# Softmax weights of a recurrent-memory transformer: one Exp after the sums, and another place for the first half's weights

## The chip, the cores and the metric

The kernel runs on one core of a Trainium2 chip. The metric is the device time of one execution in microseconds (us), lower is better. Of the engines, TensorE (PE, with its weight loads PEld) multiplies matrices, VectorE (DVE), ScalarE (ACT) and GpSimd (POOL) work on tiles, and SyncE (SP) issues DMAs.

## The reference

Two branches start from the layer-normalised input `xn` (2048 tokens of 1024 values). One is a dense GELU network. The other is an attention that goes through the tokens in 64 segments of 32, each with 8 memory tokens in front that are the output of the segment before:

```python
for s in range(n_seg):                      # 64, each needs the memory of the one before
    h = concatenate([mem, xs], axis=1)      # 8 + 32 tokens
    q, k, v = h @ Wq, h @ Wk, h @ Wv        # 32 heads of 128
    scores = where(mask, q @ k.T * Dh ** -0.5, -1e9)
    p = softmax(scores)
    o = (p @ v) @ Wo
    mem = o[:, :M]                          # 8 rows go on to the next segment
    outs.append(o[:, M:])
return x + A_ref(xn, ...) + B_ref(xn, w1, b1, w2, b2)
```

## The kernel before, in words

The GELU network comes first (some 340 us). Then 64 segments follow one another, some 21 us each. A segment takes all of Wq, Wk, Wv and Wo, cut into 64 units of 512 KB. Of these, 47 stay in SBUF; 17 are brought anew in each segment, 15 by a DMA from HBM (`Wc_*`, issued by SyncE at line 286) into six slots in turn, and 2 by VectorE, which copies them out of PSUM banks where they are kept (`copy_bits`, line 275). When a streamed unit's products are done, `unit_done` starts the next one in its slot. The order in which streamed and resident units alternate is written out by hand (`PLACED`), for four kinds of segment, `i4 = s % 4`.

A segment goes through half passes of eight units: K0, Q0, K1, Q1, V0, V1 (0 and 1 are the halves of the 32 heads), and then 16 units of Wo. 24 of a segment's tokens and the 8 memory rows are multiplied by each unit (`product`, line 832, four matmuls of 512 columns on TensorE's four column groups). The last 8 tokens of four segments are gathered and multiplied once in four segments; such a pass (`left`) takes two products per unit. They fall on K in i4 = 0, V0 in 1, Q0 and V1 in 2, Q1 and Wo in 3.

The attention's steps are put between units of the passes, each after the unit that a table names, by i4:

- `scores(u)` (lines 945 and 951): the first half's after unit `SCORES_0` of K1, the second half's in `attend`, after unit `ATTEND` of V1. The scores stand in the PSUM bank `mixed`: 160 columns (4 heads of a partition group by 40 queries, part A) and 64 columns (the keys of the gathered tokens, part B).
- `exps(u)`: ScalarE's Exp, and VectorE's minimum with two masks that hold 0 or 3e38 (lines 969 and 970).
- `sums(u)`, after unit `SUMS_0` of Q1 and `SUMS_1` of V1: TensorE sums the weights of a head over its keys and spreads the sum (978, 984); ScalarE takes Ln (989) and then Exp of the negative (992), which is the sum's reciprocal. Two heads share a matmul of `values`, so the weights are laid out as pairs in which the other head's places are zero. Before, the zero comes out of the second Exp: it runs twice, with a bias `off` of 0 or -30000 for each partition. VectorE then multiplies (1000 for A, into `pd_main`; 1004 for B).
- `values(u, rs)`, after unit `VALUES_0` of V1 and `VALUES_1` of Wo (1019, 1025, copied out at 1038).

The queries of a half are copied and transposed by `turn_q` (916 by ScalarE, 920 by VectorE, in two parts of eight heads) and `q_left` (928) into `q_home`, 640 columns of the tile `kq`. The first half's weights after Exp stand in columns 400 to 624 of the same place, so the second half's queries must wait for line 1004. At the end of Wo, in segments without gathered rows, `fold` adds the halves of a bank (1084 to 1086), line 1190 adds the rest, `put_mem` (329, 339) brings the 8 memory rows into the next segment's tokens, and four to six products of a gathered pass (`lead_products`) lie beside that.

Of the kernel before, what the change touches and what calls it, by code (L numbers as in the profile page):

```python
# [11 lines left out]
U32 = mybir.dt.uint32  # L12
F32 = mybir.dt.float32
ACT = mybir.ActivationFunctionType
# [16 lines left out]
INV_SQRT_DH = 1.0 / math.sqrt(DH)  # L31
EPS = 1e-5
PASSED = 3.0e38
NEVER = -30000.0

# [18 lines left out]
EARLY_SEGS = 7  # L56
LEAD_FIRST = 4
SCORES_0 = (6, 6, 6, 6)
SUMS_0 = (4, 4, 4, 4)
ATTEND = (0, 0, 1, 0)  # L60
VALUES_0 = ((4, 4), (4, 4), (3, 5), (4, 4))
SUMS_1 = (6, 6, 5, 7)
VALUES_1 = (5, 5, 5, 5)
LATER = 4
LAG = 3
# [55 lines left out]
def kernel(  # L121
# [62 lines left out]

    homes = [hr_home[:, 0:256], hr_home[:, 256:512]]
    small_consts = consts.tile([P, 16], BF16, name="small_consts")
    bd, off = small_consts[:, 0:4], small_consts[:, 4:8].bitcast(F32)

    def slab(place):
        if place in low:  # L190
# [6 lines left out]
    ident_mem = nc.alloc_sbuf_tensor_at("ident_mem", [P, 4, NL], BF16, offset=SCRATCH + 3712)[:, :, :]  # L197
    nc.vector.tensor_copy(out=ident_mem[:, :, :], in_=ident.rearrange("p (j t) -> p j t", j=4)[:, :, NX:SEG])
    nc.vector.memset(bd[:, :], 0.0)
    nc.vector.memset(off[:, :], NEVER)  # L200
    for j in range(4):
        q = slice(32 * j, 32 * j + 32)
        nc.vector.memset(bd[q, j:j + 1], 1.0)
        nc.vector.memset(off[q, j % 2:j % 2 + 1], 0.0)


    mask = qL[1].rearrange("p h t -> p (h t)")[:, 0:NX + GRP * 16]
# [65 lines left out]
    def copy_bits(out, in_):  # L273

        nc.vector.tensor_single_scalar(out=out, in_=in_, scalar=0, op=ALU.bitwise_or)  # L275

    def start_stream(slot):
        if not starts:
            return
        n = starts.popleft()  # L280
        unit, t = streams[n], slab(slot)
        if unit in kept_in:
            for c0, bank in kept_in[unit]:
                copy_bits(t[:, c0:c0 + 1024].bitcast(U32), bank.bitcast(U32))
        elif unit in copies:
            nc.sync.dma_start(out=t[:, :], in_=copies[unit])
        else:
            fetch(t[:, :], unit)
        stream_tiles[n], slot_of[n] = t, slot
# [447 lines left out]
    with tc.tile_pool(name="late", bufs=1) as late:  # L737
# [65 lines left out]
        for s in range(NSEG):  # L803
# [14 lines left out]
            left_v = [first or i4 == 1, first or i4 == 2]  # L818
            left_o = i4 == 3
            mover = nc.vector if s < EARLY_SEGS else nc.gpsimd  # L820
            st = {}

            def product(w, i, t, lhs, acc, seq, left=False):
                for j in range(4):
# [111 lines left out]
            def scores(u):  # L936
# [12 lines left out]
                for j in range(4):  # L949
# [3 lines left out]
                        start=False, stop=True, skip_group_check=True, tile_position=(0, 32 * j),  # L953
                    )

            def exps(u):

                if u:
                    prA = q_all[:, 512:672].rearrange("p (c q) -> p c q", q=40)
                    prB = ko_slots[1][:, 0:64, i4]  # L960
                    nc.scalar.activation(out=q_all[:, 512:672], in_=mixed[:, 0:160], func=ACT.Exp, scale=INV_SQRT_DH)
                    nc.scalar.activation(out=prB, in_=mixed[:, 160:224], func=ACT.Exp, scale=INV_SQRT_DH)  # L962
                else:
                    pr = q_all[:, 400:624]
                    nc.scalar.activation(out=pr, in_=mixed[:, 0:224], func=ACT.Exp, scale=INV_SQRT_DH)
                    prA = pr[:, 0:160].rearrange("p (c q) -> p c q", q=40)
                    prB = pr[:, 160:224]
                p = prA[:, :, NL:SEG]
                nc.vector.tensor_tensor(out=p, in0=p, in1=mask_order[:, None].to_broadcast(list(p.shape)), op=ALU.min)  # L969
                nc.vector.tensor_tensor(out=prB, in0=prB, in1=mask_left, op=ALU.min)  # L970
                st["pr", u] = prA, prB.rearrange("p (c a q) -> p c a q", a=2, q=NL)

            def sums(u):
                prA, prB = st["pr", u]
                dA = mixed[:, 0:160].rearrange("p (c q) -> p c q", q=40)
                for j in range(4):
                    q = slice(32 * j, 32 * j + 32)
                    nc.tensor.matmul(
                        dA[q, :, :], lhsT=bd[:, j:j + 1].to_broadcast([P, 32]), rhs=prA, start=True, stop=False,
                        skip_group_check=True, tile_position=(0, 32 * j),  # L980
                    )
                for j in range(4):
                    q = slice(32 * j, 32 * j + 32)
                    nc.tensor.matmul(
                        ends(dA[q, :, :]), lhsT=bd[:, j:j + 1].to_broadcast([P, 32]),
                        rhs=prB,
                        start=False, stop=True, skip_group_check=True, tile_position=(0, 32 * j),
                    )
                nc.scalar.activation(out=mixed[:, 0:160], in_=mixed[:, 0:160], func=ACT.Ln)

                for b in (1, 0):
                    nc.scalar.activation(  # L992
                        out=mixed[:, 160 * b:160 * b + 160], in_=mixed[:, 0:160], func=ACT.Exp, scale=-1.0,
                        bias=off[:, b:b + 1],
                    )
                pdA = pd_main.rearrange("p (c b q) -> p c b q", c=4, b=2)
                place = qL_slots[0] if first or VALUES_0[i4][0] < VALUES_0[i4][1] else ko_slots[0]
                pdB = q_all[:, 512:640] if u else place[:, :, i4]
                dd = mixed[:, 0:320].rearrange("p (b c q) -> p b c q", b=2, q=40)
                nc.vector.tensor_tensor(  # L1000
                    out=pdA.rearrange("p c b q -> p b c q"), in0=prA[:, None, :, :].to_broadcast([P, 2, 4, 40]),
                    in1=dd, op=ALU.mult,
                )
                nc.vector.tensor_tensor(
                    out=pdB.rearrange("p (c b a q) -> p b c a q", c=4, b=2, q=NL),
                    in0=prB[:, None, :, :, :].to_broadcast([P, 2, 4, 2, NL]),
                    in1=dd.rearrange("p b c (e q) -> p b c e q", q=NL)[:, :, :, ::4, :], op=ALU.mult,
                )
                st["pd", u] = pdA, pdB

            def values(u, rs):

                V, (pdA, pdB) = st["V", u], st["pd", u]
                av = {r: new_acc() for r in rs}
                oV = {r: av[r][:, 0:320].rearrange("p (c b q) -> p c b q", c=4, b=2) for r in rs}
                for c in range(4):
                    for r in rs:
                        q = slice(64 * r, 64 * r + 64)
                        nc.tensor.matmul(  # L1019
                            oV[r][:, c, :, :], lhsT=V[q, c * P:(c + 1) * P], rhs=pdA[q, c, :, :],  # L1020
                            start=(c == 0), stop=False, skip_group_check=True, tile_position=(64 * r, 0),
                        )
                for r in rs:
                    q = slice(64 * r, 64 * r + 64)
                    nc.tensor.matmul(
                        av[r][:, 0:320].rearrange("p (n e q) -> p n e q", n=8, q=NL)[:, :, ::4, :],
                        lhsT=VL[u][q, i4 * P:(i4 + 1) * P], rhs=pdB[q, :].rearrange("p (n a q) -> p n a q", n=8, q=NL),
                        start=False, stop=True, skip_group_check=True, tile_position=(64 * r, 0),
                    )
                for r in rs:  # L1030
                    cp = nc.vector.tensor_copy if r else nc.scalar.copy
                    h = slice(8 * r, 8 * r + 8)
                    parts = [
                        (ko[u].rearrange("p h (t s) -> p h t s", s=GRP)[:, h, :, i4], 0, NL),
                        ((outM if u else nat_home)[:, h, :], NL, 40),
                    ]
                    for out, q0, q1 in parts:
                        cp(out=out.rearrange("p (b c) q -> p c b q", b=2), in_=oV[r][:, :, :, q0:q1])  # L1038
                    let_go(av[r])
# [39 lines left out]
            def fold(ps):  # L1079
# [2 lines left out]

                here, there = [ps[:, 256 * b:256 * b + 256].rearrange("p (h e) -> p h e", e=16) for b in range(2)]
                nc.scalar.copy(out=t[0:64], in_=there[64:128])
                nc.vector.tensor_copy(out=t[64:128], in_=there[0:64])
                nc.vector.tensor_tensor(out=t[:, :, :], in0=here, in1=t[:, :, :], op=ALU.add)
                let_go(ps)
                return t
# [26 lines left out]
            at = {  # L1115
                0: [lambda: nc.vector.transpose(out=nat_home, in_=nat_home)],
            }
            at[4 if first else SUMS_0[i4]] = [lambda: sums(0)] + ([] if left_q[1] else [lambda: q_left(1)])
            if left_k[1]:
                at.setdefault(1, []).insert(0, lambda: turn_kL(psK1L, 1))  # L1120
            psQ1, psQ1L = half_pass("Q", 1, left_q[1], at, lambda ps: turn_qL(ps, 1))
# [19 lines left out]
                st["V", 0] = values_out(psV, v_home, nc.scalar.copy)  # L1141
                exps(1)

            at = {0 if first else ATTEND[i4]: [attend]}
            n0, n1 = (3, 5) if first else VALUES_0[i4]
            if n0 == n1:
                at.setdefault(n0, []).append(lambda: values(0, (0, 1)))
# [15 lines left out]
                load_left_rows(g + 2, left_rows_in[:, :])  # L1163
            at = {VALUES_1[i4]: [lambda: values(1, (0, 1))]}
            psX = new_acc()
            for n, unit in enumerate(O_UNITS):
                t = unit_tile(unit)
                if n == NPAIR and not left_o:
# [3 lines left out]
                unit_done(unit)  # L1172
                for fn in at.get(n, ()):
                    fn()
                if n == 6 and left_o:
                    st["resL"] = pd_main[:, 0:256]
                    loads.dma_start(
                        out=st["resL"], in_=resL_d[g, :, :]
                    )
# [94 lines left out]
```

## Time and profile before

| what | value |
|---|---|
| time, median of 3 runs | 1776.12 us (1768.8 to 1776.93) |
| profiled execution: its own time | 1779.09 us |
| profiled execution: span | 1777.4 us |
| TensorE busy | 1690.2 us (95%), 28374 matmuls |
| VectorE busy | 1020.6 us (57%), 2592 instructions |
| ScalarE busy | 697.1 us (39%), 1743 instructions |
| DMA moved | 593.82 MB, mean 334 GB/s over the span |
| granted TensorE clock | 0.999 |

The span goes from the first to the last instruction. Lines of the profile name an engine, a line of the kernel (L1000 is line 1000), an operation and `out<-in` by the program's names. In an order of time each line has the start and the duration in us, and in square brackets the idle time before it and what ended it. A line of waits has who waited for whom, the total in us, the number of times and the longest.

### The profile page before, as it was taken

Reading aid. Unit: us, or ns where it says so; the run is one execution under the profiler, and the core shown is the slowest. Engines: PE = TensorE matmul, PEld = TensorE weight load, DVE = VectorE, ACT = ScalarE, POOL = GpSimd, SP = SyncE. Lnnn points to the kernel's source line nnn. Section 1 sums busy time; section 2 is a strip of 40 time slices with the busy share of each in tenths; the row PEclk is TensorE's granted clock in tenths of the full one; section 3 lists DMA queues with packets and bytes.
Section 4 is the critical chain, followed back from the end, with each engine's and each line's share of the span. In section 5 each row is a group of like instructions: output and inputs, shape, how many; then the busy total and the mean of one; then the engine's idle time right before and its main releaser. Section 6 shows DMA issues by size and latency. Waiting matters only on the chain.

```text
span 1777.4 us, 65923 instructions
## 1 busy us (share of the span) xinstructions
PE 1690.2 (95%) x28374; PEld 834.6 (47%) x28374; DVE 1020.6 (57%) x2592; ACT 697.1 (39%) x1743; POOL 293.0 (16%) x590
## 2 busy tenths in 40 slices
PE   9999999998999999999999989999999999999998
PEld 5444444444444444444444444444444444444444
DVE  7657483826556555555556555555565655565554
ACT  6334251703334343334334433433333434333333
POOL 0000002403120111121211212121212111111120
PEclk9999999999999999999999999999999999999999
DMA  9455312779999999999999999999999999999997
GB/s 273 152 165 173 97 37 64 275 268 349 380 384 395 381 389 387 388 388 392 381 385 393 384 386 363 400 370 397 384 399 376 396 384 402 378 387 390 395 382 293
DMA packets 233752, 593.82 MB, mean 334 GB/s; under 512 B 58003, under 2 KB 88771, under 8 KB 233460
## 3 DMA queue, kind: packets, MB, share of 16 engines
q1 hardware_dynamic: 199680, 568.05, 84.5%
q0 software_dynamic: 16160, 15.82, 2.8%
q10 hardware_dynamic: 17620, 5.74, 1.3%
q8 instruction: 222, 3.64, 0.8%
q14 instruction: 70, 0.57, 0.1%
HBM read 573.22 MB, written 28.70 MB: 339 GB/s over the span
## 4 chain that ended last, share of the span: by engine, by line
PE 41%; DMA 25%; DVE 5%; ACT 3%; issue 1%; ACTq 0%; DVEq 0%; SPq 0%
PE acc L832 27%; PE acc L1069 11%; DMA u<-Wc_O 11%; DMA u<-Wc_Q 7%; DMA u<-Wc_V 4%; DMA u<-Wc_K 2%; PE acc L1019 1%; DVE kq L920 1%; ACT mixed L992 1%; DMA hr_home<-res_d 1%; ACT qL L886 1%; PE mixed L945 1%; DVE pd_main L1000 1%; PE mixed L329 1%; DVE kq L1190 0%
## 5 line engine op out<-in xcount | busy, mean ns | idle before, releaser
L832 PE MATMUL acc<-u,hr_home 128*32 128x512 bf16 x11520 | 756.7, 380 | 34.2 <-DMA u<-Wc_V 18.0
L832 PEld LDWEIGHTS <-hr_home 128*32 128x32 bf16 x12288 | 330.8, 97 | 335.1 <-issue 53.6
L832 PE MATMUL acc<-u,hrL 128*32 128x512 bf16 x3008 | 258.0, 380 | 0.7 <-issue 0.7
L533 PE MATMUL ps<-u 128*128 128x512 bf16 (+1 forms) x992 | 195.1, 358 | 0.6 <-DMA u<-in_B_w_dram 0.6
L886 ACT CAST d_oL<-acc 128x512 bf16<-128x512 f32 x143 | 83.1, 583 | 243.7 <-PE acc L832 223.2
L275 DVE TENSOR_SCALAR u<-kept 128x512 uint32<-128x512 uint32 x254 | 162.2, 679 | 27.0 <-PE acc L832 22.2
L1069 PE MATMUL acc<-u,d_oL 128*32 128x512 bf16 x2560 | 164.4, 380 | 9.4 <-DMA u<-Wc_O 9.3
L663 PE MATMUL ps<-u 128*128 128x512 bf16 x672 | 146.0, 379 | 0.0
L1069 PE MATMUL acc<-u,kq 128*32 128x256 bf16 (+1 forms) x2688 | 131.3, 319 | 13.4 <-DMA u<-Wc_O 10.9
L533 PEld LDWEIGHTS <-u 128*128 128x128 bf16 x992 | 91.6, 98 | 102.3 <-DMA u<-in_B_w_dram 0.8
L1000 DVE TENSOR_TENSOR pd_main<-kq,mixed 128x320 bf16<-128x320 bf16 x128 | 62.5, 488 | 124.8 <-ACT mixed L992 124.8
L1069 PEld LDWEIGHTS <-kq 128*32 128x32 bf16 x3328 | 86.7, 96 | 88.7 <-ACT kq L1038 25.8
L916 ACT CAST kq<-acc 128x256 bf16<-128x256 f32 x256 | 89.3, 375 | 99.2 <-PE acc L832 59.6
L1236 POOL DMA_DIRECT2D out_dram<-hr_home x168 | 85.5, 517 | 253.9 <-DVE hr_home L1209 253.9
L969 DVE TENSOR_TENSOR kq<-kq,mixed 128x96 bf16<-128x96 bf16 x128 | 26.2, 204 | 168.5 <-ACT kq L962 90.5
L920 DVE STREAM_TRANSPOSE kq<-kq 128x256 bf16<-128x256 bf16 x256 | 98.1, 422 | 30.7 <-ACT kq L916 30.6
L832 PEld LDWEIGHTS <-hrL 128*32 128x32 bf16 x3200 | 83.9, 97 | 55.5 <-issue 5.0
L890 ACT CAST kq<-acc 128x512 bf16<-128x512 f32 x128 | 75.2, 588 | 75.2 <-PE mixed L951 72.4
L663 PEld LDWEIGHTS <-u 128*128 128x128 bf16 x672 | 65.5, 98 | 78.8 <-DVE u L620 0.4
L612 ACT ACTIVATE u<-ps,b1col 128x512 bf16<-128x512 f32 x112 | 76.5, 684 | 65.6 <-PE ps L533 62.7
L992 ACT ACTIVATE mixed<-mixed,small_consts 128x160 f32<-128x160 f32 x256 | 94.2, 368 | 8.4
L1069 PEld LDWEIGHTS <-d_oL 128*32 128x32 bf16 x2560 | 62.1, 96 | 65.1 <-issue 14.3
(136 smaller groups left out, 1853.9 us busy)
## 6 DMA issues: line engine op xcount, KB each, us to landing
u<-Wc_K SPq DMA_DIRECT2D x256, 512.0 KB
u<-Wc_V SPq DMA_DIRECT2D x256, 512.0 KB
u<-Wc_O SPq DMA_DIRECT2D x256, 512.0 KB
u<-Wc_Q SPq DMA_DIRECT2D x192, 512.0 KB
u<-in_B_w_dram SPq DMA_DIRECT2D x28, 512.0 KB
u<-in_A_Wq_dram SPq DMA_DIRECT2D x13, 512.0 KB
u<-in_A_Wv_dram SPq DMA_DIRECT2D x12, 512.0 KB
u<-in_A_Wk_dram SPq DMA_DIRECT2D x9, 512.0 KB
```

The costliest lines, as they stand in the source:

```text
L275: nc.vector.tensor_single_scalar(out=out, in_=in_, scalar=0, op=ALU.bitwise_or)
L533: nc.tensor.matmul(ps[:, SEG * s0:SEG * s1].rearrange("p (s t) -> p s t", t=SEG), lhsT=w1_sb[fb // 2][:, kt, (fb % 2) * P:(fb % 2 + 1) * P ...
L612: nc.scalar.activation(out=xb[:, :], in_=ps[:, :], func=ACT.Identity, bias=b1col[:, fb:fb + 1], scale=1.0)
L663: nc.tensor.matmul(ps[:, :], lhsT=gts[fc // 4][:, fc % 4, t * P:(t + 1) * P], rhs=w2_sb[fc // 2][:, fc % 2, cs], start=(fc == 0), stop=(fc ...
L832: nc.tensor.matmul(o, lhsT=lhs[:, i, :], rhs=m, start=(i == seq[0]), stop=(i == seq[-1]), tile_position=(0, 32 * j),)
L886: cp(out=out, in_=ps.rearrange("p (h e) -> p h e", e=32))
L916: nc.scalar.copy(out=q_home[:, h0:h1, NL:40], in_=ps[:, 32 * h0:32 * h1].rearrange("p (h e) -> p h e", e=32))
L920: nc.vector.transpose(out=half, in_=half)
L992: nc.scalar.activation(out=mixed[:, 160 * b:160 * b + 160], in_=mixed[:, 0:160], func=ACT.Exp, scale=-1.0, bias=off[:, b:b + 1],)
L1000: nc.vector.tensor_tensor(out=pdA.rearrange("p c b q -> p b c q"), in0=prA[:, None, :, :].to_broadcast([P, 2, 4, 40]), in1=dd, op=ALU.mult,)
L1069: nc.tensor.matmul(acc[r0:r0 + rows, 0:256 * len(blocks)], lhsT=lhsT, skip_group_check=True, rhs=o_columns(t, k, blocks), start=start, sto ...
L1236: loads.dma_start(out=out_flat[rows, 256 * j:256 * j + 256], in_=res[32 * j:32 * j + NX, :])
```

## The change

Five things are done at once. The second Exp after the sums runs once, and the other head of a pair is zeroed by a factor of 0 or 1 for each partition (`of_pair`) in VectorE's scalar_tensor_tensor: with the mask for part B (in `exps`, before the sums) and with the reciprocal for part A (in `sums`). The first half's weights no longer stand in the queries' place but where their final form will stand (`pd_main` for A; a slot of `ko_slots` or `qL_slots` for B), and the second half's B in a slot of `ko_slots[1]`. The sums are called after other units, `q_left(1)` after unit 1 of Q1, and `attend` after unit 0 always. `fold` has both its copies on ScalarE. The copies of a kept unit that would start in Wo before `values(1)` are held until after it.

```diff
-SUMS_0 = (4, 4, 4, 4)
-ATTEND = (0, 0, 1, 0)
+SUMS_0 = (3, 3, 3, 2)
-SUMS_1 = (6, 6, 5, 7)
+SUMS_1 = (6, 5, 5, 6)
...
-    nc.vector.memset(off[:, :], NEVER)
+    nc.vector.memset(of_pair[:, :], 0.0)
...
-        nc.vector.memset(off[q, j % 2:j % 2 + 1], 0.0)
+        nc.vector.memset(of_pair[q, j % 2:j % 2 + 1], 1.0)
...
+    copies_back, st = [], {}
+
+    def copy_back():
+        while copies_back:
+            t, bank = copies_back.pop(0)
+            copy_bits(t.bitcast(U32), bank.bitcast(U32))
...
         if unit in kept_in:
-            for c0, bank in kept_in[unit]:
-                copy_bits(t[:, c0:c0 + 1024].bitcast(U32), bank.bitcast(U32))
+            copies_back.extend((t[:, c0:c0 + 1024], bank) for c0, bank in kept_in[unit])
+            if not st.get("hold"):
+                copy_back()
...
+            def pair_places(u):
+                left = qL_slots[0] if u == 0 and (first or VALUES_0[i4][0] < VALUES_0[i4][1]) else ko_slots[u]
+                B = left[:, :, i4]
+                both = pd_main, B
+                return both, (
+                    pd_main.rearrange("p (c b q) -> p b c q", c=4, b=2),
+                    B.rearrange("p (c b n) -> p b c n", c=4, b=2),
+                )
...
             def exps(u):
-                if u:
-                    prA = q_all[:, 512:672].rearrange("p (c q) -> p c q", q=40)
-                    prB = ko_slots[1][:, 0:64, i4]
-                    nc.scalar.activation(out=q_all[:, 512:672], in_=mixed[:, 0:160], func=ACT.Exp, scale=INV_SQRT_DH)
-                    nc.scalar.activation(out=prB, in_=mixed[:, 160:224], func=ACT.Exp, scale=INV_SQRT_DH)
-                else:
-                    pr = q_all[:, 400:624]
-                    nc.scalar.activation(out=pr, in_=mixed[:, 0:224], func=ACT.Exp, scale=INV_SQRT_DH)
...
+                st["pd", u], (pdA, pdB) = pair_places(u)
+                prA = q_all[:, 512:672].rearrange("p (c q) -> p c q", q=40) if u else pdA[:, 1]
+                nc.scalar.activation(
+                    out=prA, in_=mixed[:, 0:160].rearrange("p (c q) -> p c q", q=40), func=ACT.Exp, scale=INV_SQRT_DH
+                )
+                nc.scalar.activation(
+                    out=pdB[:, 1], in_=mixed[:, 160:224].rearrange("p (c n) -> p c n", c=4), func=ACT.Exp,
+                    scale=INV_SQRT_DH,
+                )
...
-                nc.vector.tensor_tensor(out=prB, in0=prB, in1=mask_left, op=ALU.min)
+                for b in range(2):
+                    nc.vector.scalar_tensor_tensor(
+                        out=pdB[:, b], in0=mask_left.rearrange("p (c n) -> p c n", c=4), scalar=of_pair[:, b:b + 1],
+                        in1=pdB[:, 1], op0=ALU.mult, op1=ALU.min,
+                    )
...
             def sums(u):
...
-                        rhs=prB,
+                        rhs=pdB[:, j % 2],
...
                 nc.scalar.activation(out=mixed[:, 0:160], in_=mixed[:, 0:160], func=ACT.Ln)
-                for b in (1, 0):
-                    nc.scalar.activation(
-                        out=mixed[:, 160 * b:160 * b + 160], in_=mixed[:, 0:160], func=ACT.Exp, scale=-1.0,
-                        bias=off[:, b:b + 1],
+                nc.scalar.activation(out=mixed[:, 0:160], in_=mixed[:, 0:160], func=ACT.Exp, scale=-1.0)
+                for b in range(2):
+                    nc.vector.scalar_tensor_tensor(
+                        out=pdA[:, b], in0=prA, scalar=of_pair[:, b:b + 1], in1=dA, op0=ALU.mult, op1=ALU.mult
                     )
...
+                for b in range(2):
+                    w = pdB[:, b].rearrange("p c (a q) -> p c a q", a=2)
+                    nc.vector.tensor_tensor(out=w, in0=w, in1=ends(dA), op=ALU.mult)
...
                 nc.scalar.copy(out=t[0:64], in_=there[64:128])
-                nc.vector.tensor_copy(out=t[64:128], in_=there[0:64])
+                nc.scalar.copy(out=t[64:128], in_=there[0:64])
...
-            at[4 if first else SUMS_0[i4]] = [lambda: sums(0)] + ([] if left_q[1] else [lambda: q_left(1)])
+            if not left_q[1]:
+                at.setdefault(1, []).append(lambda: q_left(1))
+            at.setdefault(4 if first else SUMS_0[i4], []).append(lambda: sums(0))
...
-            at = {0 if first else ATTEND[i4]: [attend]}
+            at = {0: [attend]}
...
+            st["hold"] = True
             for n, unit in enumerate(O_UNITS):
...
+                if n == VALUES_1[i4]:
+                    st["hold"] = False
+                    copy_back()
```

More of the change, by code (lines that the diff above doesn't have):

```diff
@@ L33 @@
 PASSED = 3.0e38
-NEVER = -30000.0
 NX = 24
@@ L186 @@
     small_consts = consts.tile([P, 16], BF16, name="small_consts")
-    bd, off = small_consts[:, 0:4], small_consts[:, 4:8].bitcast(F32)
+    bd, of_pair = small_consts[:, 0:4], small_consts[:, 4:8].bitcast(F32)
     def slab(place):
@@ L820 @@
             mover = nc.vector if s < EARLY_SEGS else nc.gpsimd
-            st = {}
+            st.clear()
             def product(w, i, t, lhs, acc, seq, left=False):
@@ L954, in scores @@
                     )
-            def exps(u):
-                if u:
-                    prA = q_all[:, 512:672].rearrange("p (c q) -> p c q", q=40)
-                    prB = ko_slots[1][:, 0:64, i4]
-                    nc.scalar.activation(out=q_all[:, 512:672], in_=mixed[:, 0:160], func=ACT.Exp, scale=INV_SQRT_DH)
-                    nc.scalar.activation(out=prB, in_=mixed[:, 160:224], func=ACT.Exp, scale=INV_SQRT_DH)
-                else:
-                    pr = q_all[:, 400:624]
-                    nc.scalar.activation(out=pr, in_=mixed[:, 0:224], func=ACT.Exp, scale=INV_SQRT_DH)
-                    prA = pr[:, 0:160].rearrange("p (c q) -> p c q", q=40)
-                    prB = pr[:, 160:224]
+            def pair_places(u):
[6 more added lines that the diff above has]
+                )
@@ L968, in exps @@
                 p = prA[:, :, NL:SEG]
                 nc.vector.tensor_tensor(out=p, in0=p, in1=mask_order[:, None].to_broadcast(list(p.shape)), op=ALU.min)
-                nc.vector.tensor_tensor(out=prB, in0=prB, in1=mask_left, op=ALU.min)
-                st["pr", u] = prA, prB.rearrange("p (c a q) -> p c a q", a=2, q=NL)
+                for b in range(2):
[3 more added lines that the diff above has]
+                    )
@@ L973, in sums @@
+                st["pr", u] = prA, pdA, pdB
             def sums(u):
-                prA, prB = st["pr", u]
+                prA, pdA, pdB = st["pr", u]
                 dA = mixed[:, 0:160].rearrange("p (c q) -> p c q", q=40)
@@ L989, in sums @@
                 nc.scalar.activation(out=mixed[:, 0:160], in_=mixed[:, 0:160], func=ACT.Ln)
-                for b in (1, 0):
-                    nc.scalar.activation(
-                        out=mixed[:, 160 * b:160 * b + 160], in_=mixed[:, 0:160], func=ACT.Exp, scale=-1.0,
-                        bias=off[:, b:b + 1],
-                    )
[L996 to L1009, printed above, removed]
+                nc.scalar.activation(out=mixed[:, 0:160], in_=mixed[:, 0:160], func=ACT.Exp, scale=-1.0)
+                for b in range(2):
+                    nc.vector.scalar_tensor_tensor(
+                        out=pdA[:, b], in0=prA, scalar=of_pair[:, b:b + 1], in1=dA, op0=ALU.mult, op1=ALU.mult
+                    )
+                for b in range(2):
+                    w = pdB[:, b].rearrange("p c (a q) -> p c a q", a=2)
+                    nc.vector.tensor_tensor(out=w, in0=w, in1=ends(dA), op=ALU.mult)
             def values(u, rs):
@@ L1019, in values @@
                         nc.tensor.matmul(
-                            oV[r][:, c, :, :], lhsT=V[q, c * P:(c + 1) * P], rhs=pdA[q, c, :, :],
+                            oV[r][:, c, :, :], lhsT=V[q, c * P:(c + 1) * P], rhs=pdA[q, 80 * c:80 * c + 80].rearrange("p (b q) -> p b q", b=2),
                             start=(c == 0), stop=False, skip_group_check=True, tile_position=(64 * r, 0),
```

## The prediction

> **What bounds the kernel now.** The page comes first. TensorE is busy 95% of the span, VectorE 57%, ScalarE 39%, and the DMA row stands at 9 from slice 9 on. The chain that ended last names TensorE and the weight stream together:
>
> ```profile
> PE 41%; DMA 25%; DVE 5%; ACT 3%; issue 1%; ACTq 0%; DVEq 0%; SPq 0%
> ```
>
> Single segments (busy time by stretch, columns as in the answer's head; five segments, i4 = 0, 1, 2, 3, 0) show that the DMA engines never rest, at 361 to 402 GB/s:
>
> ```profile
> 925.50:946.10 20.60, 20.17 (x419) 9.84 (x422) 12.25 (x32) 8.78 (x24) 5.02 (x10) 1.00 0.98 361
> 946.10:966.60 20.50, 18.68 (x386) 9.49 (x386) 11.51 (x31) 7.70 (x22) 3.17 (x6) 1.00 1.02 402
> 966.60:987.10 20.50, 20.15 (x418) 10.45 (x417) 12.78 (x33) 8.76 (x24) 3.49 (x7) 1.00 1.02 401
> 987.10:1008.80 21.70, 21.38 (x436) 10.80 (x434) 11.41 (x30) 8.50 (x23) 4.03 (x8) 1.00 1.02 400
> ```
>
> From 440 to 1750 us the mean is 387 GB/s; at 402 the same bytes would take 1310 x 387/402 = 1261 us. TensorE's own floor: its groups of four matmuls start 0.216 us apart (40 matmuls in 2.34 us), and adding up in the trace what any two starts are further apart than that gives 126 us of standing still in those 1310 us, 66 of them for a streamed unit. Without those, 1244 us. Two servers, each some 96% used, feed each other through six slots, so I let half of any TensorE time saved or lost reach the end; the bounds are none of it (DMA alone decides) and all of it.
>
> The other 60 us are what the change can touch. The view of waits, TensorE from 440 to 1750 us, shows the ends of these stalls (each row understates: a matmul is written as 0.38 us long):
>
> ```profile
> PE mixed L329 <- DVE kq L1190: 4.3, 22, 0.5
> PE acc L1019 <- DVE pd_main L1000: 4.0, 16, 0.3
> PE mixed L945 <- DVE kq L920: 2.3, 15, 0.2
> ```
>
> By starts of matmuls these are 10.9 us before L329, 14.1 before L945 (11.8 of them in the second half's scores), and 17.1 before L1019: 7.4 for L1000, 4.2 for ScalarE's L890, 5.5 without a name.
>
> One i4 = 2 segment in order of time has nearly all that the change touches:
>
> ```profile
> 972.82 0.22 PE L951 MATMUL mixed<-kq,d_oL 128*32 128x64 bf16 x4
> ...
> 973.09 0.36 ACT L965 ACTIVATE kq<-mixed 128x224 bf16<-128x224 f32 x1 [1.40 <-PE mixed L951]
> 973.34 0.58 ACT L886 CAST d_oL<-acc 128x512 bf16<-128x512 f32 x1
> 973.48 0.20 DVE L969 TENSOR_TENSOR kq<-kq,mixed 128x96 bf16<-128x96 bf16 x1 [0.81 <-ACT kq L965]
> 973.60 0.18 DVE L970 TENSOR_TENSOR kq<-kq,mixed 128x64 bf16<-128x64 bf16 x1
> ...
> 974.14 0.26 PE L978 MATMUL mixed<-kq,small_consts 128*32 128x160 bf16 x4
> ...
> 974.52 0.29 ACT L989 ACTIVATE mixed<-mixed 128x160 f32<-128x160 f32 x1 [0.60 <-PE mixed L984]
> 974.84 0.77 ACT L992 ACTIVATE mixed<-mixed,small_consts 128x160 f32<-128x160 f32 x2
> ...
> 975.64 0.49 DVE L1000 TENSOR_TENSOR pd_main<-kq,mixed 128x320 bf16<-128x320 bf16 x1 [0.98 <-ACT mixed L992]
> 976.05 0.43 DVE L1004 TENSOR_TENSOR qL<-kq,mixed 128x128 bf16<-128x128 bf16 x1
> 976.52 0.37 ACT L916 CAST kq<-acc 128x256 bf16<-128x256 f32 x1 [0.60 <-DVE qL L1004]
> ```
>
> The last line is the wait for the first half's weights in the queries' place: 64 times 0.6 us on ScalarE (28.2 + 10.2 us in the waits).
>
> **Part by part.** *Weights out of the queries' place.* L916's wait goes, the second transpose L920 ends about 0.5 us earlier, and the second half's scores, 0.19 us late in the mean (11.8 us / 62), stop waiting. Taken: 10.5 us. In i4 = 2 they also move up one unit, which stays covered: L920 would end near 977.1, scores start at 977.5. q_left(1), one 0.213 us VectorE copy, passes the sums' operations in VectorE's queue; its reader is those scores, 3 us later.
>
> *One Exp after the Ln.* Two take 0.77 us; one without the bias I put at L989's 0.288 us (same shape, no pointer operand; upper end 0.368, L992's own). Then VectorE: two products of 160 elements instead of L1000's 320 (0.488 us), by 1.04 ns per element between L1004 (0.287, 128 elements) and L1000, 0.32 us each, started 0.08 us before the former's end as L1004 does; two of 64 instead of one of 128. From the end of the sums to pdA: before 1.71 us, after 0.10 + 0.29 + 0.03 + 0.29 + 0.03 + 0.32 + 0.24 = 1.30; to all weights 1.73 instead of 2.06. With the sums' new units this ends L1000's 7.4 us, and L890, queued behind the Exps on ScalarE, goes 0.45 us earlier. Taken: 12 of 17.1 us.
>
> *Fold by ScalarE.* L1085 is serial already (29.4 us of waiting for L1084). A second 0.369 us copy behind L1084, overlapping by some 0.09, instead of 0.418: L1086 and L1190 come 0.14 us earlier, 47 times: 6.5 us of the 10.9.
>
> *The masks.* Where L970 was one operation, two with a 0/1 factor stand, written with a stride of four elements. The trace has no such operation. Nearest rows: L970 strided (second half) 0.29 us, dense (first half) 0.18. I take 0.29. The first half gets a second Exp as well, as the second half has: 0.31 and 0.32 us, 0.20 apart. In the segment above, counted from the scores' end (973.04): Exps 0.08 to 0.59, L969 0.62 to 0.83, factors 0.74 to 1.04 and 0.95 to 1.25, sums 0.10 later at 1.35 (L978 waits for L970 too: 3.8 us in TensorE's weight loads). The sums stood at 1.10 and are now called one unit earlier, 0.90: TensorE, with every weight product queued behind, stands 0.45 us. In i4 = 1 the same, in i4 = 0 (medians over 13 segments) 0.23, in i4 = 3 none. In the second half the factors end at 1.71 against L970's 1.50: sums at 1.81 where TensorE comes at 1.60 in i4 = 0 and 3: 0.21 each, 0.1 in i4 = 1, whose V units mostly come late anyway. Sum: 0.23 + 0.45 + 0.45 + 0.21 + 0.21 + 0.10 = 1.65 us in four segments, 15.5 times: 25.6 us; less the segments already late there for a streamed unit, 20. Ends: with dense 0.18 us operations 0.5 x 15.5 = 8; without overlap between them 39.
>
> The row on overlap: L970 starts 0.12 us after L969, which lasts 0.20. The Trainium skill, "VectorE: DVE Perf Modes", section "The DRAIN you can't avoid", says that the next operation waits until the pipe is empty, which would make the sum by the upper end, 39; the same sentence exempts operations that are not held, and this trace agrees with the exemption.
>
> *Small ones.* Strided weights: L1025 0.276 us (first half) against 0.218, L984 0.219 against 0.193: 0.08 us a segment, 5 us. exps(0) now writes pd_main, out of which i4 = 3 stores rows (L1215): the store's last packet ends 1.2 us after to 1.6 before the next segment's first Exp, so it waits in some of 15: 2 us (ends 0 and 8). rows_out of K1 comes 0.27 us later on ScalarE; its reader is 3 us away. In i4 = 0 the kept unit's two copies (1.29 us) move behind values(1)'s; they send no DMA, and their reader, unit 15, starts 0.4 us after their new end: nothing, or 0.9 us a time if that cover goes.
>
> Sum on TensorE: -10.5 - 12 - 6.5 + 20 + 5 + 2 = -2 us; half of it, -1. The profiled execution took 1779.1 us (span 1777.4 and 1.7 around it), so 1778; it lies 3.0 above the median of the runs shown, 1776.1, so **1775**.
>
> **The rivals.** *Faster:* the factors take 0.18 to 0.22 us and the sums hardly wait (8 us): -14 us on TensorE, and as stalls lie between passes, where slots come free late, most of it reaches the end: about 1762. For: the best segments run at 402 GB/s, so the stream can follow. Against: the strided row. *Slower:* the factor, with its pointer and a mask in PSUM, takes longer. Each 0.1 us more per operation makes the sums 0.2 us later at five places in four segments, 15 us on TensorE; at 0.45 us each 24 us more, all of it passed on since the stream is not short then: about 1795. It decides from roughly 0.39 us an operation. *Slower by the rule of the Trainium skill named above:* no overlap on VectorE, +17 us, half to all of it: about 1788. *The change doesn't do its work:* the stream alone decides, TensorE then waits for DMA what it no longer waits for data: within 2 us, inside the forecast.
>
> **How the numbers follow.** A measurement of this kernel tells about 0.5% (8.9 us) from no change. Forecast, with the last rival, 0.39; faster 0.34; slow factor 0.23; no overlap 0.04. The range leaves out the fastest passes below 1760 and the slow factor's upper part above 1789. The forecast's own range is 1768 to 1784.
>
> **What would show it.** L916 no longer waiting; L945 starting without L920 behind it; L992's line one Exp of 0.29 us; a new wait of L978 on the factors, 0.2 to 0.45 us in both halves; the factor at 0.29 us; DMA still at 1.0. Wrong if L978 doesn't wait (faster), if the factor lasts over 0.39 us, or if stream waits grow by all that the others lose.

## The result: 0.9% slower, and TensorE now waits before the sums

The changed kernel takes 1791.9 us in the median of 5 runs (1788.7 to 1793.6) against 1776.1 us of the kernel before; the ratio is 1.0088, with a 95% interval of 1.0069 to 1.0108. In a second comparison (after_again, below) it was 1.0096 (1.0066 to 1.0127). The profiled execution took 1789.2 us, its span is 1787.4 us.

TensorE is as busy as before (95%), VectorE somewhat more, ScalarE less:

```profile
PE 1691.1 (95%) x28354; PEld 822.4 (46%) x28374; DVE 1067.9 (60%) x2928; ACT 660.4 (37%) x1727; POOL 292.1 (16%) x590
```

The view of waits of the changed kernel, from 440 to 1750 us (who waited for whom, total us, times, longest), has a line that the kernel before did not have: L998, the first matmul of the sums, waits for L987, the mask's factor. It stands there for the matmuls (PE) and for the weight loads ahead of them (PEld), in three tiles. The lines for L945 and L1000, which the prediction showed, have no counterpart among TensorE's.

```profile
PE mixed L998 <- DVE d_oL L987: 11.9, 33, 0.5
PE mixed L998 <- DVE kq L987: 8.1, 31, 0.3
PE mixed L998 <- DVE qL L987: 7.1, 16, 0.4
```

In order of time, an i4 = 2 segment of the changed kernel. The first line is the end of the scores, the second has the five units (20 matmuls) that lie before the sums:

```profile
976.56 0.22 PE L958 MATMUL mixed<-kq,d_oL 128*32 128x64 bf16 x4
976.59 1.27 PE L839 MATMUL acc<-u,hr_home 128*32 128x512 bf16 x20
976.83 0.30 ACT L977 ACTIVATE pd_main<-mixed 128x160 bf16<-128x160 f32 x1 [1.39 <-PE mixed L958]
977.03 0.31 ACT L980 ACTIVATE qL<-mixed 128x64 bf16<-128x64 f32 x1
...
977.37 0.20 DVE L985 TENSOR_TENSOR pd_main<-pd_main,mixed 128x96 bf16<-128x96 bf16 x1 [0.96 <-ACT qL L980]
977.50 0.75 DVE L987 SCALAR_TENSOR_TENSOR qL<-mixed,small_consts,qL 128x64 bf16<-128x64 bf16 x2
...
978.30 0.25 PE L998 MATMUL mixed<-pd_main,small_consts 128*32 128x160 bf16 x4 [0.44 <-DVE qL L987]
...
978.71 0.29 ACT L1009 ACTIVATE mixed<-mixed 128x160 f32<-128x160 f32 x1 [0.94 <-PE mixed L1004]
```

The two factors take 0.75 us one after the other. The sums start 1.52 us after the scores' end (976.78). Five units of 0.216 us after 976.59 TensorE had nothing left before them: it could have come at 977.67 and came at 978.30. Over the whole stretch from 440 to 1750 us, TensorE's starts before the sums lie 42 us further apart than a unit takes; in the kernel before none do. By place, in the mean: in the first half 0.43 us for i4 = 0, 0.63 for 1, 0.60 for 2 and 0.06 for 3; in the second half 0.43, 0.20, none and 0.38.

A finer account helps with what follows: over 52 segments of the steady part (the 9th to the 60th), each matmul's start is subtracted from the next one's, and the differences are added up by the steps that they lead to and lie in. A part of each figure is the ordinary time between two starts; what counts is the difference between the kernels. In us per segment, with the ratios beside them (the experiments are told below):

| kernel | to and in the sums | to and in the scores | to and in the values | to put_mem | sum of these against before | ratio of times (95%) |
|---|---|---|---|---|---|---|
| before | 0.52 | 1.08 | 1.22 | 0.43 | 0 | 1 |
| changed | 1.24 | 0.78 | 1.05 | 0.39 | +0.21 | 1.0088 (1.0069 to 1.0108) |
| masks_first | 1.29 | 0.72 | 1.05 | 0.39 | +0.21 | 1.0083 (1.0063 to 1.0102) |
| old_units | 0.92 | 0.85 | 1.10 | 0.39 | +0.01 | 1.0016 (0.9999 to 1.0033) |
| masks_early | 0.98 | 0.74 | 1.05 | 0.39 | -0.10 | 1.0025 (1.0012 to 1.0039) |
| late_units | 0.62 | 0.98 | 1.10 | 0.39 | -0.16 | 0.9999 (0.9987 to 1.0012) |
| place_alone | 0.53 | 0.92 | 1.20 | 0.42 | -0.18 | 0.9991 (0.9976 to 1.0006) |
| raw_apart | 0.80 | 0.80 | 1.05 | 0.39 | -0.21 | 1.0001 (0.9984 to 1.0018) |
| two_masks | 0.60 | 0.81 | 1.05 | 0.38 | -0.40 | 0.9975 (0.9960 to 0.9989) |

So the change did save TensorE 0.30 us a segment at the scores, 0.17 at the values and 0.04 at put_mem, some 33 us in 64 segments. It paid 0.72 us a segment, 46 us in 64, before the sums.

### The profile page after: what moved, and what is told of

The parts are those of the page before. It is cut to its first block, busy times and chain, and to the rows that moved or that the text cites. A ratio compares the mean times of both kernels' runs of the same rounds, so it can differ in the third digit from the quotient of the medians.

```text
span 1787.4 us, 66562 instructions
## 1 busy us (share of the span) xinstructions
PE 1691.1 (95%) x28354; PEld 822.4 (46%) x28374; DVE 1067.9 (60%) x2928; ACT 660.4 (37%) x1727; POOL 292.1 (16%) x590
## 4 chain that ended last, share of the span: by engine, by line
PE 63%; DMA 24%; DVE 6%; ACT 4%; issue 2%; ACTq 0%; DVEq 0%; POOL 0%; POOLq 0%; SPq 0%
PE acc L839 26%; PE ps L540 11%; PE acc L1077 11%; DMA u<-Wc_O 8%; PE ps L670 8%; DMA u<-Wc_Q 6%; DMA u<-Wc_K 6%; DMA u<-Wc_V 3%; PE ps L701 3%; PE acc L1027 1%; PE mixed L998 1%; DVE d_oL L987 1%; ACT kq L1046 1%; PE mixed L952 1%; DVE u L273 1%
## 5 line engine op out<-in xcount | busy, mean ns | idle before, releaser
L273 DVE TENSOR_SCALAR u<-kept 128x512 uint32<-128x512 uint32 x254 | 161.7, 677 | 26.8 <-PE acc L839 25.6
L927 DVE STREAM_TRANSPOSE kq<-kq 128x256 bf16<-128x256 bf16 x256 | 98.0, 421 | 30.0 <-ACT kq L923 30.0
L923 ACT CAST kq<-acc 128x256 bf16<-128x256 f32 x256 | 82.8, 375 | 70.8 <-PE acc L839 68.5
L1171 POOL DMA_DIRECT2D hr_home<-res_d x57 | 31.9, 560 | 334.4 <-PE acc L839 334.4
L608 ACT ACTIVATE u<-u 128x512 bf16<-128x512 bf16 x112 | 69.8, 623 | 8.7 <-DVE u L627 8.3
L1046 DVE CAST kq<-acc 128x64 bf16<-128x64 f32 (+1 forms) x128 | 35.7, 361 | 54.1 <-PE acc L1033 54.1
```

The costliest lines, as they stand in the source:

```text
L608: nc.scalar.activation(out=sg[:, :], in_=u[:, :], func=ACT.Sigmoid, scale=GELU_C)
L923: nc.scalar.copy(out=q_home[:, h0:h1, NL:40], in_=ps[:, 32 * h0:32 * h1].rearrange("p (h e) -> p h e", e=32))
L927: nc.vector.transpose(out=half, in_=half)
```

## The experiments

Theory W: the loss is TensorE's wait for the two factor operations. Theory V: it is the longer VectorE work itself, its strides and the held copies, wherever the sums stand. Theory M: the wait would only move if the sums stood later. Ratios are to the kernel before on the same chip.

**old_units.** The sums go back to the units of before.

```diff
-SUMS_0 = (3, 3, 3, 2)
-SUMS_1 = (6, 5, 5, 6)
+SUMS_0 = (4, 4, 4, 4)
+SUMS_1 = (6, 6, 5, 7)
```

> The changed kernel with the sums back at the units of before (SUMS_0 4, 4, 4, 4; SUMS_1 6, 6, 5, 7). Theory W (TensorE's wait at L998 for the two factor operations L987 is the loss, 42.6 us of standing still between 440 and 1750 us): one unit of 0.216 us more cover at four places in four segments takes the wait to some 24 us, and half to two thirds of the 18 us saved reach the end: 1780 to 1783 us, ratio to before about 1.003. Theory V (the longer VectorE work itself, its strides and the moved copies delay everything, wherever the sums stand): no change from 1.009, 1790 us or more.

Measured: 1780.3 us, 1.0016. The stall before the sums, counted by starts further apart than a unit, went from 42.0 to 23.4 us. That is the figure that W gave. No VectorE operation was changed, so V falls for most of the loss.

**late_units.** The sums stand as late as the tables allow.

```diff
-SUMS_0 = (3, 3, 3, 2)
-SUMS_1 = (6, 5, 5, 6)
+SUMS_0 = (5, 6, 6, 4)
+SUMS_1 = (7, 6, 5, 7)
```

> The changed kernel with the sums so late that the factors are done when TensorE comes, as far as the tables allow (SUMS_0 5, 6, 6, 4; SUMS_1 7, 6, 5, 7). W: the wait at L998 falls from 42.6 us to under 8 us, what the change saves elsewhere shows, 1768 to 1776 us, ratio 0.995 to 1.000. V: 1790 us as before. Theory M (the wait only moves: later sums make the second half's scores and the values wait for VectorE's products instead): the stalls before the scores and the values grow by 20 us or more and the time stays at 1783 to 1792 us.

Measured: 1776.1 us, 0.9999; stall before the sums 4.3 us, and the matmul rows of L998 are gone from the waits, with only rows of weight loads left:

```profile
PEld L998 <- DVE kq L987: 12.4, 27, 0.5
PEld L998 <- DVE d_oL L987: 10.3, 31, 0.4
PEld L998 <- DVE qL L987: 3.9, 13, 0.3
```

This is again what W expected. Of M there is a part: the scores take 0.98 us a segment instead of 0.78. The queries' transposes (L927) start 0.45 us after ScalarE's copy in the median instead of 0.20, with VectorE's products now just ahead of them.

**raw_apart.** Part B's Exp goes into a tile of its own, so that the second factor does not write over what the first one reads.

```diff
-                    out=pdB[:, 1], in_=mixed[:, 160:224].rearrange("p (c n) -> p c n", c=4), func=ACT.Exp,
-                    scale=INV_SQRT_DH,
+                    out=raw_left[:, :], in_=mixed[:, 160:224], func=ACT.Exp, scale=INV_SQRT_DH,
...
-                        in1=pdB[:, 1], op0=ALU.mult, op1=ALU.min,
+                        in1=raw_left.rearrange("p (c n) -> p c n", c=4), op0=ALU.mult, op1=ALU.min,
```

> The changed kernel with part B's Exp written to a tile of its own, dense, so that the second factor no longer writes over what the first one reads. W, with the two factors' order as its cause: their starts come closer than the 0.39 us of now, to 0.25 to 0.30, the sums' wait falls by 0.10 to 0.15 us at each of five to six places in four segments (8 to 13 us of TensorE), time 1783 to 1788 us. If the second factor waits for the engine and not for the data, the starts stay 0.39 us apart and the time stays near 1791 us.

Measured: 1775.3 us, 1.0001, a lower time than expected. The starts of the two factors are 0.195 us apart (median of 128 pairs) instead of 0.390, though each takes as long as before (0.354 us). In the changed kernel each of the 128 second factors starts 0.034 to 0.037 us after the first one's end. The dense Exp also takes 0.224 us instead of 0.31. One i4 = 2 segment:

```profile
978.24 0.22 ACT L981 ACTIVATE raw_left<-mixed 128x64 bf16<-128x64 f32 x1
978.49 0.20 DVE L985 TENSOR_TENSOR pd_main<-pd_main,mixed 128x96 bf16<-128x96 bf16 x1 [0.87 <-ACT raw_left L981]
978.61 0.55 DVE L987 SCALAR_TENSOR_TENSOR qL<-mixed,small_consts,raw_left 128x64 bf16<-128x64 bf16 x2
...
979.21 0.25 PE L998 MATMUL mixed<-pd_main,small_consts 128*32 128x160 bf16 x4
```

The pair takes 0.55 us instead of 0.75. The stall before the sums fell from 42.0 to 15.5 us: with the pair and the Exp, 0.28 us less at five to six places in four segments, 22 to 26 us in 62.

**two_masks.** The mask is multiplied by the factor once, at the start, so that a plain minimum of two SBUF tiles is left; Exp as in raw_apart.

```diff
-                    nc.vector.scalar_tensor_tensor(
-                        out=pdB[:, b], in0=mask_left.rearrange("p (c n) -> p c n", c=4), scalar=of_pair[:, b:b + 1],
-                        in1=pdB[:, 1], op0=ALU.mult, op1=ALU.min,
-                    )
+                    nc.vector.tensor_tensor(
+                        out=pdB[:, b], in0=raw_left.rearrange("p (c n) -> p c n", c=4),
+                        in1=masks_of[b].rearrange("p (c n) -> p c n", c=4), op=ALU.min,
+                    )
```

> The changed kernel with the two masks multiplied by the 0/1 factor once at the start (in SBUF) and part B's Exp in a tile of its own, so that each factor operation is a plain minimum without pointer and without PSUM. W: each takes 0.15 to 0.30 us instead of 0.357, the starts are 0.13 us apart, the wait at L998 falls from 42.6 us to 5 to 12 us with the units of the changed kernel left as they are, and the time to 1764 to 1776 us, ratio 0.993 to 1.000. V: the other strided operations, the fold and the held copies remain, time 1785 us or more.

Measured: 1774.3 us, 0.9975; stall before the sums 0.1 us with the units of the changed kernel. The two operations, 0.300 us each with their starts 0.135 us apart, are done in 0.45 us, and L1000 (here the sums' first matmul) follows its units without a wait, before the second of them ends at 973.20:

```profile
972.63 0.20 DVE L987 TENSOR_TENSOR pd_main<-pd_main,mixed 128x96 bf16<-128x96 bf16 x1 [0.87 <-ACT raw_left L983]
972.75 0.45 DVE L989 TENSOR_TENSOR qL<-raw_left,pair_masks 128x64 bf16<-128x64 bf16 x2
973.02 0.25 PE L1000 MATMUL mixed<-pd_main,small_consts 128*32 128x160 bf16 x4
```

This is what W expected: fold, held copies, the reciprocal's factor and the strided products all remain, and the loss is gone.

The run changes one thing more than the lengths. In the changed kernel the factors read the mask out of `mixed`, the PSUM bank that the sums are written into, and there no sum starts before its second factor has ended (0 of 123; in raw_apart 0 of 124). In two_masks the factors read SBUF alone, and 33 of 124 sums do. That the bank is the link is seen in place_alone (below): its minimum L977 and the sums' first matmul L988 share no tile but `mixed`, and the weight load ahead of L988 still waits for L977:

```profile
PEld L988 <- DVE qL L977: 4.3, 16, 0.3
```

If the sums of two_masks had to wait for the second operation's end as well, they would come 8.7 us later in all (an estimate from its own starts and ends, with the 0.054 us that the changed kernel's sums start after it). So two_masks owes some of its gain to the place of the masks; raw_apart, with the masks still in the bank, does without that part.

**masks_early and masks_first.** The opposite test: two_masks, whose VectorE work is short, with the first half's sums called too early. Nothing but the table is changed, in two doses.

```diff
-SUMS_0 = (3, 3, 3, 2)
+SUMS_0 = (1, 1, 1, 1)      # masks_early; (0, 0, 0, 0) in masks_first
```

> The kernel two_masks (whose sums wait 0.1 us in all) with the first half's sums called two units earlier still (SUMS_0 1, 1, 1, 1 instead of 3, 3, 3, 2), and nothing else: no VectorE operation is added or made longer, TensorE alone comes too early. W (a wait of TensorE before the sums costs, whatever makes it): the sums wait 25 to 40 us between 440 and 1750 us and the time rises by 12 to 22 us, to 1786 to 1796 us. V (the cost of the change lies in its longer VectorE work): no loss against two_masks, 1772 to 1777 us.

> The kernel two_masks with the first half's sums right after unit 0 of Q1 (SUMS_0 0, 0, 0, 0): one unit, 0.216 us, less cover at three to four places in four segments than masks_early, whose sums waited 11.8 us. W: the wait is 21 to 26 us and the time 8 to 14 us above two_masks, with no VectorE operation changed. V: no more than 3 us above it.

Measured: masks_early 1778.7 us, 1.0025; masks_first 1789.3 us, 1.0083. The stalls by starts further apart than a unit are 11.8 and 28.2 us, lower than expected for masks_early, because there the first sums start without the factors and part of the wait lies between the sums' own matmuls, and a little higher than expected for masks_first (21 to 26). With that part, the table's column has +0.46 and +0.77 us a segment against the kernel before. The time of masks_early lies below the 1786 to 1796 us that W gave, that of masks_first 14.6 us above two_masks on the same chip. masks_first pays at the sums what the changed kernel pays, without a pointer operation ahead of them, and loses the same. The two largest waits of its sums:

```profile
PEld L1000 <- issue: 37.3, 62, 0.7
PE mixed L1000 <- DVE pd_main L987: 16.6, 48, 0.4
```

**after_again and two_masks_again.** Both unaltered, on one chip with masks_first.

> The changed kernel unaltered, beside the two others on one chip: 1789 to 1794 us, ratio 1.007 to 1.011, sums' wait 42 us.

> The kernel two_masks unaltered, on the same chip: ratio 0.996 to 0.999, sums' wait under 1 us. If 42 us less of waiting at the sums are the whole loss, it stands 14 to 20 us below the changed kernel.

Measured: 1789.1 us, 1.0096; and 1774.7 us, 0.9998 (0.9979 to 1.0017). The difference is 14.4 us, as expected; the ratio of two_masks is a little above what was expected. That two_masks beats the kernel before is not settled: 0.9975 on one chip, 0.9998 on the other.

**place_alone.** The kernel before with only the first half's weights in their final places, and q_left(1) earlier.

```diff
-                    pr = q_all[:, 400:624]
-                    nc.scalar.activation(out=pr, in_=mixed[:, 0:224], func=ACT.Exp, scale=INV_SQRT_DH)
+                    slots = qL_slots[0] if first or VALUES_0[i4][0] < VALUES_0[i4][1] else ko_slots[0]
+                    prA = pd_main.rearrange("p (c b q) -> p b c q", c=4, b=2)[:, 1]
+                    prB = slots[:, :, i4].rearrange("p (c b n) -> p b c n", c=4, b=2)[:, 1]
...
-            at[4 if first else SUMS_0[i4]] = [lambda: sums(0)] + ([] if left_q[1] else [lambda: q_left(1)])
+            if not left_q[1]:
+                at.setdefault(1, []).append(lambda: q_left(1))
+            at.setdefault(4 if first else SUMS_0[i4], []).append(lambda: sums(0))
```

> The kernel before with one part of the change: the first half's weights in their final places instead of the queries' place, and q_left(1) after unit 1; two Exps with the bias, one minimum, fold on VectorE and the units of the sums as before. Its own theory: ScalarE's L916 no longer waits, the stall before the scores falls from 14.1 us to under 4 us, the sums hardly wait (one strided minimum is done at 1.04 us, TensorE comes at 1.11), time 1771 to 1776 us, ratio 0.997 to 0.999. The rival (the second queries were covered by V0's eight units anyway and the stream takes what is saved): within 1 us of before.

Measured: 1772.5 us, 0.9991 (0.9976 to 1.0006). The stall before the scores fell from 14.1 to 6.4 us, the sums wait 0.1 us, and L916's waits for L1004 are gone from ScalarE's; the gain is not told from none.

**fold_alone.** The kernel before with both of fold's copies on ScalarE.

```diff
-                nc.vector.tensor_copy(out=t[64:128], in_=there[0:64])
+                nc.scalar.copy(out=t[64:128], in_=there[0:64])
```

> The kernel before with both copies of fold on ScalarE and nothing else. Theory: the stall before put_mem falls by 2 to 6 us in 48 segments, time lower by 1 to 3 us, hardly told from none. Rival: ScalarE's second copy holds up what is queued behind it and the time rises by 1 us or more.

Measured: 1775.9 us, 1.0003 (0.9992 to 1.0013). The stall before put_mem fell from 12.3 to 10.1 us; no change in the time.

**masks_values.** two_masks with the first half's values one unit later.

```diff
-VALUES_0 = ((4, 4), (4, 4), (3, 5), (4, 4))
+VALUES_0 = ((5, 5), (5, 5), (3, 5), (5, 5))
```

> The kernel two_masks with the first half's values one unit later in V1 (VALUES_0 5 instead of 4, but for i4 = 2), for the wait of the values for ScalarE's copy of V0. If TensorE's waits for data are still worth having, the stall before the values falls from 13.5 us to some 8 us and the time by 0 to 3 us against two_masks; if the weight stream takes all that is saved, no change (1772 to 1776 us).

Measured: 1777.8 us, 1.0009 (0.9997 to 1.0021), slower than either expectation, though not told from the kernel before, and two_masks itself was not run on this chip. The stall before the values stayed at 13.7 us, and the one before Wo's units that need their results rose from 8.9 to 15.6 us: a later step seems to have taken the wait over.

## Why the prediction was wrong, by its own steps

**The masks are the step that failed.** The prediction saw the wait and put it where it is: the sums one unit earlier, the factors 0.10 us too late even for the old unit, L998 held by the second factor. It took 20 us of TensorE, with 39 as the upper end. Measured: 42 us from 440 to 1750 us, 46 by the table over all 64 segments. Its sum by place was 0.23 + 0.45 + 0.45 in the first half and 0.21 + 0.21 + 0.10 in the second, 1.65 us in four segments; at the same six places, in the same order, 0.43 + 0.63 + 0.60 and 0.43 + 0.38 + 0.20 were measured, 2.67. The places were right and each came 0.10 to 0.22 us too low. The deduction from 25.6 to 20 us for segments that are late there anyway had no counterpart: 2.67 times 15.5 is 41. Two sizes were off. Each factor took 0.357 us instead of 0.29, the row of the strided L970; and the second started 0.390 us after the first instead of 0.21, the overlap having been read off L969 and L970, which do not touch the same data. The second factor writes over what the first one reads and waits for its end; raw_apart, which takes that away (and makes the Exp dense), shows 0.195. The sums were to come 1.35 us after the scores and came after 1.52.

**Place.** 10.5 us were taken for the scores; the stall fell from 14.1 to 2.4 us, by the table, which has the short pauses too, by 19. That step was right, and L916 (now L923) waits for VectorE no more.

**One Exp.** L1010 takes 0.288 us, as taken. The products by the reciprocal and 0 or 1 take 0.375 to 0.378 us instead of 0.32, and in the first half, where the second one again writes over what the first one reads, their starts are some 0.42 us apart instead of 0.24; in the second half 0.30. Of the 12 us taken at the values, 5.4 came by the count of starts (18.7 to 13.3 us); with the pauses between the values' own matmuls, too short for that count, it is 0.17 us a segment, 11 us in 64.

**Fold.** 6.5 us taken, 2.4 measured (12.3 to 9.9, where the prediction counted 10.9). The overlap of 0.09 us was not there: the second copy starts 0.380 us after the first, which lasts 0.368.

**Half of it reaches the end.** This step failed too. The prediction's sum on TensorE was -2 us; the table's is +13, and half of that would have given some 1783 us, inside the range. Where the steps' sum lies below the kernel before (by 0.10 to 0.40 us a segment, 6 to 26 us), the time stays within 0.25% of it; in the two kernels where it lies above by 0.21 us, 13 us in 64 segments, the time rises by 14 to 17 us, in full. The likely reading is that the kernel before already stands about where the weight stream sets the end, so that a loss passes and a gain does not. masks_early fits it least: its sum is 0.10 us lower and its time 0.25% higher. The prediction's last rival, in which TensorE waits for the stream what it no longer waits for data, would then hold for gains alone. That the stream takes gains back is seen in the starts that wait for a unit's DMA: 63 us before, 72 in two_masks, 56 in the changed kernel.

**The rivals.** The slow factor came true at a duration below the point from which it was to decide (0.357 us against 0.39), because the lost overlap adds to it. The one without overlap, by the rule of the Trainium skill ("VectorE: DVE Perf Modes", "The DRAIN you can't avoid"), had the right place and nearly the right sum, 39 against 42 us, but 0.04 of the chance. The sum was near in part by luck: L985 and the first factor do overlap (their starts are 0.12 us apart, and L985 takes 0.20), and each factor is longer than that sum assumed. The trace of before agreed with the rule's exemption for neighbours without a wait between them; here every second factor waits for VectorE's own semaphore, and in raw_apart, where no second factor waits for the first, the starts are 0.195 us apart, as by the exemption.

The change's other steps could not be told apart in the time: place_alone and fold_alone each lie within their intervals of no change, and the single Exp and the held copies were not tried alone.

## What to carry to other kernels

When two operations take the place of one, look whether the second writes what the first reads or writes: then they follow each other with their full durations, and a row of two independent neighbours is no measure for them. Cost a new operation inside the stretch that another engine waits for against that stretch's slack, not against its own engine's idle time: VectorE was idle 40% of the span here, and waits for it of 0.2 to 0.6 us, at six places in four segments, cost 46 us of TensorE. Look also at what the operation reads: here a mask kept in the bank that the next matmuls write made them wait for the operations that read it. And in a kernel that stands near the rate of its weight stream, do not count on half: here a loss of 13 us counted in full, and gains of up to 26 us hardly at all.

## What the runs showed of the hardware

In the changed kernel a scalar_tensor_tensor with a pointer factor and one operand in PSUM takes 0.357 us for 64 strided elements (raw_apart 0.354), in two_masks a plain minimum of two SBUF tiles with the same output takes 0.300. In the kernel before, L970's minimum of 64 elements takes 0.18 us where it is dense and 0.29 where it has a stride of four elements. On ScalarE the Exp of 64 columns takes 0.224 us into a dense tile and 0.31 to 0.32 into one with a stride of four elements. In these runs two VectorE operations of that size in a row start 0.135 us (plain) or 0.195 us (pointer) apart when neither touches the other's data, and 0.390 when the second writes over the first one's input. ScalarE's two Exps of the second half start 0.196 us apart though each lasts 0.31; the two copies of fold, which go to different halves of the partitions, 0.380 us apart, without overlap.
